# Expert 2's weight loads moved to the end of attention, in a fused attention and top-1 mixture-of-experts kernel

## The chip, the cores and the metric

The kernel runs on one core of a Trainium2 chip. The metric is the device time of one execution in microseconds (us). A profile of one execution is used beside it; its times count from the first instruction, and its span is a little shorter than the device time.

## The reference

Linear attention over 8 batches, 8 heads, 576 positions of 64 values, with an RMS norm; then a mixture of 8 experts in which each of the 4608 tokens goes to one expert.

```python
def _attn_ref(q, k, v, g_norm):
    kv = np.einsum('bhsd,bhse->bhde', k, v)
    out = np.einsum('bhsd,bhde->bhse', q, kv)
    rms = np.sqrt(np.mean(out * out, axis=-1, keepdims=True) + 1e-06)
    return (out / rms * g_norm).astype(np.float32)

def _moe_ref(x, w_gate, w1, w2):          # x: 4608 x 512, w1: 8 x 512 x 1024, w2: 8 x 1024 x 512
    logits = x @ w_gate
    expert_idx = np.argmax(logits, axis=1)
    ...                                   # gate_w: softmax probability of that expert
    for e in range(E):
        mask = expert_idx == e
        h = np.maximum(x[mask] @ w1[e], 0.0)
        out[mask] = gate_w[mask, None] * (h @ w2[e])
    return out
```

Inputs, weights and output are float32.

## The kernel before

Attention runs in 36 steps of 128 tokens. Each finished group of tokens is routed: its rows are scattered by GpSimd to a scratch tensor in HBM, sorted by expert. The experts then gather their rows from there, 128 at a time, transpose them on TensorE (`flip`), multiply by W1 (`one`), apply the ReLU on ScalarE, multiply by W2 (`two`), scale on VectorE (`ys`), and scatter the result rows to the output (`put`).

Experts 0 and 1 are split. Their first three tiles of 128 rows (`Early`, `j0` and `j1`) come from tokens routed early and are gathered before attention ends, through `rowa`. Their other two tiles (`jobs[0]`, `jobs[1]`) and all five tiles of experts 2 to 7 are gathered through `rowi`, which needs every scatter. A last job takes rows beyond the capacity of 608 per expert.

The weights of an expert are 2 MB for W1 and 2 MB for W2 in float32. They are loaded by the queue of SyncE into staging buffers and cast to float16 by `half1` (W1, on ScalarE or VectorE) and `half2` (W2). There is one staging buffer for each of W1 and W2 (`ws1`, `ws2`); expert 1 alone is staged in buffers that the attention inputs k and v leave free (`stage_in`). With `hold`, a one-column memset on VectorE stands before the load, so that the load is issued only when VectorE has come to that place of its program.

```python
        def stage1(self, hold=False):
            self.s1 = P_w.tile([128, 4, F], F32, tag="ws1", bufs=1, name="ws1")
            if hold:
                nc.vector.memset(self.s1[:, 0, 0:1], 0.0)
            nc.sync.dma_start(
                self.s1, moe_w1[self.e, :, :].rearrange("o (t p) f -> p (o t) f", p=128)
            )

        def stage2(self, hold=False):
            self.s2 = P_w.tile([128, 8, D], F32, tag="ws2", bufs=1, name="ws2")
            if hold:
                nc.vector.memset(self.s2[:, 0, 0:1], 0.0)
            nc.sync.dma_start(
                self.s2, moe_w2[self.e, :, :].rearrange("o (t p) d -> p (o t) d", p=128)
            )

        def stage_in(self, pool):

            self.s1, self.s2 = [], []
            for dst, src, tag in ((self.s1, moe_w1, "k"), (self.s2, moe_w2, "v")):
                rows = src[self.e, :, :].rearrange("o (t p) f -> p (o t) f", p=128)
                n = rows.shape[1] // 2
                for m in range(2):
                    t = pool.tile([128, n, rows.shape[2]], F32, tag=tag, bufs=2, name="ws")
                    nc.sync.dma_start(t, rows[:, n * m:n * m + n, :])
                    dst.extend([t[:, kk, :] for kk in range(n)])
...
        def half1(self, eng, kk):     # casts a quarter of W1
...
        def half2(self, kk, eng=None):  # casts a quarter of W2, on ScalarE if no engine is named
...
```

The hooks of the attention steps (`at(last, s, ...)` runs at the end of step `s`):

```python
                for t in range(G):
                    at(last, (33, 34, 34, 35)[t] if g0 == 0 else 35, rt.scatter, t)
                    if g0 == 0 and t == 3:
                        for u in range(AT):
                            at(last, 35, gather_early, 1, u)
        for t in range(AT):
            at(late, 30 + t, gather_early, 0, t)

        at(last, 19, W[0].stage1)
        at(last, 21, W[0].stage2)
        at(last, 30, W[1].stage_in, PA)
        for kk in range(4):
            at(last, (26, 27, 28, 30)[kk], W[0].half1, nc.scalar, kk)
        for kk in range(2):
            at(last, 31 + kk, W[0].half2, kk)

```

The steps, and what follows them:

```python
        j0, j1 = early
        for s in range(36):
            op = x_mm(s)
            for fn in mid[s]:
                fn()
            if s + 2 < 36:
                qt = x_qt(s + 2)
            elif s == 34:
                j0.alloc()
                xp = PSA.tile([128, 2, 1024], F16, tag="kvp", bufs=1, name="xp")
                xp2 = PSA.tile([128, 1024], F16, tag="qtp", bufs=1, name="xp2")
                j0.flip(0, xp[:, 0, :])
                j0.flip(1, xp[:, 1, :])
            else:
                j0.flip(2, xp2)
            rest = x_norm(s, op)
            if s + 2 < 36:
                x_qs(s + 2, qt)
            elif s == 34:
                j0.turned(0, xp[:, 0, :])
                j0.turned(1, xp[:, 1, :])
            else:
                j0.turned(2, xp2)
            for fn in late[s]:
                fn()
            rest()
            for fn in last[s]:
                fn()


        j0.one(0, "op")
        PSA.tile([128, 2, 512], F32, tag="op", bufs=2, name="skipped")
        W[0].half2(2)
        j0.one(1, "kvp")
        j0.one(2, "op")
        W[0].half2(3)
        j0.one(3, "kvp")
        tail.ranks()
        for kk in range(2):
            W[1].half1(nc.scalar, kk)
...
        tail.send()
        for t in range(2):
            tail.scatter(t)
        for t in range(AT):
            j0.where(t)
        yp0 = PSA.tile([128, D], F32, tag="qtp", bufs=1, name="yp")
        j0.two(0, yp0)
...
        j0.done(0, yp0)
        yp = PSA.tile([128, D], F32, tag="misc", bufs=1, name="yp")
        j0.two(1, yp)
        j0.done(1, yp)
        xp = PSA.tile([128, 2, 1024], F16, tag="kvp", bufs=1, name="xp")
        xp2 = PSA.tile([128, 2, 1024], F16, tag="op", bufs=2, name="xp2")[:, 0, :]
        for t in range(AT):
            j1.flip(t, xp[:, t, :] if t < 2 else xp2)
        for t in range(AT):
            j1.turned(t, xp[:, t, :] if t < 2 else xp2)
            j1.where(t)
        W[1].half1(nc.scalar, 2)
        W[1].half1(nc.vector, 3)
        yp = PSA.tile([128, D], F32, tag="qtp", bufs=1, name="yp")
        j0.two(2, yp)
        for t in range(2):
            gather(xe_bufs[2 * AT + t], rowi[:, 0, AT + t:AT + t + 1])
        j0.done(2, yp)
        for t in range(2):
            gather(xe_bufs[2 * AT + 2 + t], rowi[:, 1, AT + t:AT + t + 1])
        W[2].stage1(hold=True)
        W[2].stage2(hold=True)
        for m in range(4):
            j1.one(m, ("op", "kvp")[m % 2])
            if m < 2:
                W[1].half2(m)
        for kk in (2, 3):
            W[1].half2(kk, nc.vector)
```

The jobs:

```python
            def flip(self, t):        # transposes of two tiles, then per tile a copy to xt on VectorE
            ...
            def one(self, ws, f):     # 4 matmuls; every second f a ReLU of two on ScalarE
            ...
            def two(self, t):         # 8 matmuls, then ys on VectorE and put on GpSimd
            ...
        for t in range(AT):
            if t == 2:
                jobs[0].flip(0)
            banks.reverse()
            yp = PSA.tile([128, D], F32, tag=banks[0], bufs=1, name="yp")
            j1.two(t, yp)
            j1.done(t, yp)
        for t in range(CT):
            gather(jobs[2].xe[t], rowi[:, 2, t:t + 1])

        table = left_over_table()
        for n in range(len(order)):
            job = jobs[n]
            nxt = jobs[n + 1] if n + 1 < len(order) else None
            flips = list(range(0, nxt.nt, 2)) if nxt is not None else []

            casts = {0: None, 2: 2, 3: 1, len(order) - 1: None}.get(n, 0)
            coming = list(range(CT)) if 0 < n < len(order) - 3 else []
            if n == 4:
                for _ in table:
            ...
            for ws in range(job.halves):
                for f in range(8):
                    job.one(ws, f)
                    if n in (2, 3):
                        next(table, None)
                    if n == 2 and ws == 0 and f in (3, 7):
                        W[2].half2(2 + f // 4)
                        if f == 7:
                            W[3].stage2()
                    step = 8 * ws + f
                    if coming and (step in (1, 5, 7, 11, 13) if n > 1 else f in (1, 3, 5, 6, 7)):
                        next_row(n + 2, coming.pop(0), job, ws, f)
                    if ws == (0 if n == 3 else job.halves - 1) and f in (2, 4, 6) and flips:
                        nxt.flip(flips.pop(0))
                    if casts == ws and f % 2 == 1:
                        W[n + 1].half1(nc.vector, f // 2)
                        if f == 7 and n + 2 < len(order):
                            W[n + 2].stage1()
            for kk in range(max(job.nt, 4)):
                if kk < job.nt:
                    job.two(kk)
                if casts == 2 and kk < 4:
                    W[n + 1].half1(nc.vector, kk)
                    if kk == 3 and n + 2 < len(order):
                        W[n + 2].stage1()
                if n > 0 and kk < (2 if n == 1 else 4) and nxt is not None:
                    W[n + 1].half2(kk)
                if n > 1 and kk == 3 and n + 2 < len(order):
                    W[n + 2].stage2()
```

[...]

Of the kernel before, what the change touches and what calls it, by code (L numbers as in the profile page):

```python
# [28 lines left out]
def kernel(  # L29
# [11 lines left out]
    nc = tc.nc  # L41
# [102 lines left out]
    class Weights:  # L144
# [11 lines left out]
        def stage2(self, hold=False):  # L156
            self.s2 = P_w.tile([128, 8, D], F32, tag="ws2", bufs=1, name="ws2")
            if hold:
                nc.vector.memset(self.s2[:, 0, 0:1], 0.0)
# [4 lines left out]
        def stage_in(self, pool):  # L164

            self.s1, self.s2 = [], []
            for dst, src, tag in ((self.s1, moe_w1, "k"), (self.s2, moe_w2, "v")):
                rows = src[self.e, :, :].rearrange("o (t p) f -> p (o t) f", p=128)
                n = rows.shape[1] // 2
                for m in range(2):  # L170
                    t = pool.tile([128, n, rows.shape[2]], F32, tag=tag, bufs=2, name="ws")
                    nc.sync.dma_start(t, rows[:, n * m:n * m + n, :])
                    dst.extend([t[:, kk, :] for kk in range(n)])
# [59 lines left out]
    with tc.manual_schedule(engines=by_hand):  # L233
# [402 lines left out]
        for P, g0, G in groups + [(3, 0, 4), (3, 4, 3)]:  # L636
# [11 lines left out]
            else:  # L648
# [4 lines left out]
                for t in range(G):  # L653
                    at(last, (33, 34, 34, 35)[t] if g0 == 0 else 35, rt.scatter, t)
                    if g0 == 0 and t == 3:
                        for u in range(AT):
                            at(last, 35, gather_early, 1, u)
# [5 lines left out]
        at(last, 30, W[1].stage_in, PA)  # L663
# [41 lines left out]
        for s in range(36):  # L705
# [11 lines left out]
            else:  # L717
                j0.flip(2, xp2)
# [6 lines left out]
            else:  # L725
                j0.turned(2, xp2)
# [3 lines left out]
            for fn in last[s]:  # L730
                fn()


        j0.one(0, "op")
        PSA.tile([128, 2, 512], F32, tag="op", bufs=2, name="skipped")
        W[0].half2(2)
        j0.one(1, "kvp")
        j0.one(2, "op")
        W[0].half2(3)
        j0.one(3, "kvp")  # L740
# [39 lines left out]
        W[2].stage1(hold=True)  # L780
        W[2].stage2(hold=True)
# [209 lines left out]
        for t in range(CT):  # L991
            gather(jobs[2].xe[t], rowi[:, 2, t:t + 1])

        table = left_over_table()
        for n in range(len(order)):
# [4 lines left out]
            casts = {0: None, 2: 2, 3: 1, len(order) - 1: None}.get(n, 0)  # L1000
# [6 lines left out]
            for ws in range(job.halves):  # L1007
                for f in range(8):
# [3 lines left out]
                    if n == 2 and ws == 0 and f in (3, 7):  # L1012
                        W[2].half2(2 + f // 4)
                        if f == 7:
                            W[3].stage2()
# [3 lines left out]
                    if ws == (0 if n == 3 else job.halves - 1) and f in (2, 4, 6) and flips:  # L1019
                        nxt.flip(flips.pop(0))  # L1020
# [57 lines left out]
```

## Time and profile before

| | |
|---|---|
| device time, median of 3 runs | 291.94 us (291.26 to 292.26) |
| span of the profiled execution | 284.7 us |
| TensorE matmul (PE) busy | 260.6 us, 92% |
| VectorE (DVE) busy | 162.1 us, 57% |
| ScalarE (ACT) busy | 155.9 us, 55% |
| GpSimd (POOL) busy | 159.3 us, 56% |
| moved by DMA | 85.73 MB, mean 301 GB/s |
| weight loads (SyncE) | 16 of 2048 KB and 4 of 1024 KB, median 11.2 and 11.7 us from issue to landing |

How to read it: the span covers stages with different limits, so a busy share says little of any one of them. The profile cuts the span into 40 slices of about 7.1 us and gives each a digit, the busy share in tenths; "PEclk" is the clock that TensorE was granted, "DMA" the busy share of the 16 DMA engines. In the table of waits a line says which engine and line of the kernel waited for what, with the sum in us, the number of waits and the longest. In a timeline a line gives start and duration in us, engine, line of the kernel, operation, output and input, the count of merged instructions, and in brackets the idle time before them and what ended it. L886 is `flip`, L909 `one`, L928 `two`, L937 `ys`, L182 `half1` on VectorE, L152 and L160 the loads of W1 and W2, L592 the scatter, L199 a gather.

### The profile page before, as it was taken

What the parts mean: (1) busy time and instruction counts of PE and PEld (TensorE: products, weight loads), DVE (VectorE), ACT (ScalarE), POOL (GpSimd) and SP (SyncE); (2) the same over time, 40 slices, a digit from 0 to 9 for tenths busy, and PEclk for the clock granted to TensorE, in tenths of its full rate; (3) what the DMA queues carried; (4) which work ended last, traced back from release to release, by engine and by line L of the source; (5) the groups of instructions that cost most, each with busy time, mean ns of one, the idle gap of its engine ahead of it and who ended that gap; (6) DMA issues with size and microseconds to landing.
All of it is one profiled execution on the core that took longest, in us unless ns stands there. A gap on an engine that the chain in (4) does not pass through costs nothing.

```text
span 284.7 us, 7172 instructions
## 1 busy us (share of the span) xinstructions
PE 260.6 (92%) x2832; PEld 183.9 (65%) x2832; DVE 162.1 (57%) x438; ACT 155.9 (55%) x295; POOL 159.3 (56%) x227
## 2 busy tenths in 40 slices
PE   8979999999999996699889999997979999999992
PEld 3668888888988885545447675673554765746651
DVE  6024677785979778756224767826263545545141
ACT  1135676676666888696503472750736362563721
POOL 3123206666757658877747888874675755124042
PEclk9979999999999999999979999999999999999999
DMA  7999979997999999424994499699999997959222
GB/s 259 373 389 390 391 247 353 327 395 242 397 408 395 396 344 346 162 82 134 341 398 136 135 359 342 219 360 389 385 357 373 328 410 247 398 224 306 115 111 79
DMA packets 34756, 85.73 MB, mean 301 GB/s; under 512 B 3738, under 2 KB 3998, under 8 KB 34721
## 3 DMA queue, kind: packets, MB, share of 16 engines
q1 hardware_dynamic: 26592, 65.10, 63.9%
q0 software_dynamic: 6848, 18.96, 18.0%
q10 hardware_dynamic: 1280, 1.20, 1.3%
q8 instruction: 23, 0.38, 0.5%
q14 instruction: 13, 0.10, 0.1%
HBM read 71.71 MB, written 14.98 MB: 304 GB/s over the span
## 4 chain that ended last, share of the span: by engine, by line
DMA 19%; PE 18%; issue 8%; POOL 5%; DVE 3%; ACT 1%; POOLq 1%; DVEq 0%
DMA ws<-in_moe_w_dram 8%; PE yp L928 8%; DMA out_dram<-ys,idx 8%; PE hp L909 7%; POOL out_dram L216 3%; DMA xe<-xs_scratch,rowi 2%; DVE w1e L182 2%; PE xp L886 2%; POOL xs_scratch L592 1%; PE yp L506 1%; DMA xs_scratch<-xg,sli 1%; DVE xt L890 1%; POOL xe L199 1%; ACT ht L918 0%; POOLq L1073 0%
## 5 line engine op out<-in xcount | busy, mean ns | idle before, releaser
L918 ACT ACTIVATE ht<-hp 128x608 f16<-128x608 f32 (+2 forms) x60 | 38.1, 639 | 60.7 <-PE hp L909 60.7
L216 POOL DMA_INDIRECT out_dram<-ys,idx x41 | 43.1, 1051 | 50.2 <-DVE ys L937 40.1
L928 PE MATMUL yp<-w2e,ht 128*128 128x512 f16 (+1 forms) x280 | 62.1, 379 | 1.9 <-DVE ys L937 1.9
L909 PE MATMUL hp<-xt,w1e 128*128 128x304 f16 (+2 forms) x480 | 62.9, 283 | 0.9 <-ACT ht L918 0.8
L909 PEld LDWEIGHTS <-w1e 128*128 128x128 f16 x480 | 44.9, 98 | 14.3 <-issue 2.0
L928 PEld LDWEIGHTS <-ht 128*128 128x128 f16 (+1 forms) x280 | 28.9, 103 | 32.0 <-issue 2.2
L369 PE MATMUL op<-kvs,qts 128*128 128x144 f32 (+1 forms) x320 | 46.9, 301 | 2.7 <-DVE xg L409 1.7
L937 DVE TENSOR_SCALAR ys<-yp,xe 128x512 f32<-128x512 f32 (+1 forms) x35 | 26.2, 750 | 38.1 <-PE yp L928 38.1
L592 POOL DMA_INDIRECT xs_scratch<-xg,sli x36 | 35.5, 987 | 14.2 <-issue 13.9
L369 PEld LDWEIGHTS op<-kvs,qts 128*128 128x128 f32 (+1 forms) x320 | 38.2, 181 | 5.9 <-DVE xg L409 2.0
L199 POOL DMA_INDIRECT xe<-xs_scratch,rowi x34 | 36.6, 1076 | 9.3 <-issue 4.6
L194 ACT CAST w2e<-ws 128x1024 f16<-128x1024 f32 x32 | 31.5, 1040 | 14.2 <-DMA ws<-in_moe_w_dram 14.2
L395 DVE TENSOR_REDUCE ms<-sq 128x8 f32<-128x512 f32 x36 | 24.6, 684 | 13.9 <-ACT sq L390 13.0
L390 ACT ACTIVATE sq<-op 128x512 f32<-128x512 f32 x36 | 21.4, 594 | 15.3 <-PE op L369 15.3
L283 POOL COPY qp<-q 128x512 f32<-128x512 f32 x32 | 19.3, 616 | 17.0 <-DMA q<-in_q_dram 16.9
L182 DVE TENSOR_SCALAR w1e<-ws,g 128x1024 f16<-128x1024 f32 x29 | 20.5, 748 | 10.5 <-DMA ws<-in_moe_w_dram 10.5
L409 DVE TENSOR_TENSOR xg<-op,rinv 128x512 f16<-128x512 f32 x36 | 24.5, 681 | 0.0
L354 ACT COPY qts<-qtp 128x512 f32<-128x512 f32 x36 | 21.0, 584 | 5.6 <-PE qtp L347 5.4
L347 PE MATMUL qtp<-cf,qp 128*128 128x128 f32 x144 | 22.9, 282 | 0.4 <-issue 0.4
L300 PE MATMUL kvp<-v,k 64*64 64x64 f32 x1152 | 23.2, 225 | 0.0
L890 DVE COPY xt<-xp 128x512 f16<-128x512 f16 x35 | 13.5, 420 | 16.9 <-PE xp L886 16.9
L300 PEld LDWEIGHTS kvp<-v,k 64*64 64x64 f32 x1152 | 19.6, 136 | 5.0 <-issue 5.0
(115 smaller groups left out, 267.4 us busy)
## 6 DMA issues: line engine op xcount, KB each, us to landing
ws<-in_moe_w_dram SPq DMA_DIRECT2D x16, 2048.0 KB, 11.2
q<-in_q_dram SPq DMA_DIRECT2D x8, 1152.0 KB, 13.1
k<-in_k_dram SPq DMA_DIRECT2D x7, 1152.0 KB, 7.6
v<-in_v_dram SPq DMA_DIRECT2D x7, 1152.0 KB, 10.4
ws<-in_moe_w_dram SPq DMA_DIRECT2D x4, 1024.0 KB, 11.7
k<-in_k_dram SPq DMA_DIRECT2D x2, 576.0 KB, 5.2
v<-in_v_dram ACTq DMA_DIRECT2D x2, 576.0 KB, 8.2
out_dram<-ys,idx POOLq DMA_INDIRECT x41, 5.2
```

The lines of the kernel that those rows point to most:

```text
L182: eng.tensor_scalar(self.w1[:, kk, :], st, g2, 1.0, op0=ALU.mult, op1=ALU.mult,)
L194: copy(self.w2[:, 2 * kk:2 * kk + 2, :], self.s2[:, 2 * kk:2 * kk + 2, :])
L199: return nc.gpsimd.indirect_dma_start(out=xe.bitcast(I32), out_offset=None, in_=xs.ap() if src is None else src, in_offset=IndirectOffsetO ...
L216: nc.gpsimd.indirect_dma_start(out=view, out_offset=IndirectOffsetOnAxis(ap=idx, axis=0), in_=ys, in_offset=None, bounds_check=N - 1, oob_ ...
L300: nc.tensor.matmul(kvst[b][64 * ip:64 * ip + 64, c, 64 * i2:64 * i2 + 64], ld["k", b][ps, i, cs], ld["v", b][ps, i, cs], start=(j == 0), s ...
L369: nc.tensor.matmul(op[ts, c, 144 * i2:144 * i2 + 144], qts[s][:, 2 * i2 + c, ts], kvs[:, 2 * c + i2, :], start=True, stop=True,)
L395: nc.vector.reduce_sum(ms, sq, axis=AXX)
L592: put_xs = nc.gpsimd.indirect_dma_start(out=xs_views[9 * self.P + self.g0 + t], out_offset=IndirectOffsetOnAxis(ap=self.sli[:, t:t + 1], a ...
L909: nc.tensor.matmul(self.hp[:, f % 2, 0:wd], self.w.w1[:, kk, f * 128:(f + 1) * 128], self.xt[:, kk, ws * wd:(ws + 1) * wd], start=(kk == 0 ...
L918: nc.scalar.activation(self.ht[f // 4][:, r:r + 2, ws * wd:(ws + 1) * wd], self.hp[:, :, 0:wd], ACTF.Relu,)
L928: nc.tensor.matmul(yp[ps, :], self.ht[f // 4][:, f % 4, t * 128:t * 128 + self.rows[t]], self.w.w2[:, f, :], start=(f == 0), stop=(f == 7),)
L937: nc.vector.tensor_scalar(ys[ps, :], yp[ps, :], self.xe[t][ps, 514:516].bitcast(F32), None, op0=ALU.mult,)
```

## The change

Expert 2's W1 is loaded at the end of step 34 instead of after the gathers of expert 1, and its W2 as soon as the staging buffer is free of expert 0's. To make room, expert 1's W2 is held to the end of step 33, and expert 1's three early gathers go ahead of three scatters. The cast of expert 2's W1 moves from the second part of expert 1 to that of expert 0, so that expert 3's W1 can be loaded during expert 1, behind the gathers of expert 2, which are themselves issued a tile earlier; the later casts and loads move up in the same way. The third transpose group of expert 0's early rows moves from step 35 to the end of step 34, and its four products alternate over the PSUM banks in the other order. The change is meant to use the time in which the DMA engines carry little, at the end of attention and under expert 1.

The diff:

```diff
--- before.py
+++ after.py
@@ -153,24 +153,27 @@
                 self.s1, moe_w1[self.e, :, :].rearrange("o (t p) f -> p (o t) f", p=128)
             )
 
-        def stage2(self, hold=False):
+        def stage2(self):
             self.s2 = P_w.tile([128, 8, D], F32, tag="ws2", bufs=1, name="ws2")
-            if hold:
-                nc.vector.memset(self.s2[:, 0, 0:1], 0.0)
             nc.sync.dma_start(
                 self.s2, moe_w2[self.e, :, :].rearrange("o (t p) d -> p (o t) d", p=128)
             )
 
-        def stage_in(self, pool):
-
-            self.s1, self.s2 = [], []
-            for dst, src, tag in ((self.s1, moe_w1, "k"), (self.s2, moe_w2, "v")):
-                rows = src[self.e, :, :].rearrange("o (t p) f -> p (o t) f", p=128)
-                n = rows.shape[1] // 2
-                for m in range(2):
-                    t = pool.tile([128, n, rows.shape[2]], F32, tag=tag, bufs=2, name="ws")
-                    nc.sync.dma_start(t, rows[:, n * m:n * m + n, :])
-                    dst.extend([t[:, kk, :] for kk in range(n)])
+        def stage_in(self, pool, src, tag, hold=False):
+
+            dst = []
+            rows = src[self.e, :, :].rearrange("o (t p) f -> p (o t) f", p=128)
+            n = rows.shape[1] // 2
+            for m in range(2):
+                t = pool.tile([128, n, rows.shape[2]], F32, tag=tag, bufs=2, name="ws")
+                if hold:
+                    nc.vector.memset(t[:, 0, 0:1], 0.0)
+                nc.sync.dma_start(t, rows[:, n * m:n * m + n, :])
+                dst.extend([t[:, kk, :] for kk in range(n)])
+            if src is moe_w1:
+                self.s1 = dst
+            else:
+                self.s2 = dst
 
         def half1(self, eng, kk):
             if kk == 0:
@@ -652,15 +655,17 @@
                 at(late, s + 2, rt.send)
                 for t in range(G):
                     at(last, (33, 34, 34, 35)[t] if g0 == 0 else 35, rt.scatter, t)
-                    if g0 == 0 and t == 3:
+                    if g0 == 0 and t == 0:
                         for u in range(AT):
-                            at(last, 35, gather_early, 1, u)
+                            at(last, 34, gather_early, 1, u)
         for t in range(AT):
             at(late, 30 + t, gather_early, 0, t)
 
         at(last, 19, W[0].stage1)
         at(last, 21, W[0].stage2)
-        at(last, 30, W[1].stage_in, PA)
+        at(last, 30, W[1].stage_in, PA, moe_w1, "k")
+        at(last, 33, W[1].stage_in, PA, moe_w2, "v", True)
+        at(last, 34, W[2].stage1)
         for kk in range(4):
             at(last, (26, 27, 28, 30)[kk], W[0].half1, nc.scalar, kk)
         for kk in range(2):
@@ -714,30 +719,30 @@
                 xp2 = PSA.tile([128, 1024], F16, tag="qtp", bufs=1, name="xp2")
                 j0.flip(0, xp[:, 0, :])
                 j0.flip(1, xp[:, 1, :])
-            else:
-                j0.flip(2, xp2)
             rest = x_norm(s, op)
             if s + 2 < 36:
                 x_qs(s + 2, qt)
             elif s == 34:
                 j0.turned(0, xp[:, 0, :])
                 j0.turned(1, xp[:, 1, :])
-            else:
-                j0.turned(2, xp2)
             for fn in late[s]:
                 fn()
             rest()
             for fn in last[s]:
                 fn()
-
-
-        j0.one(0, "op")
+            if s == 34:
+                j0.flip(2, xp2)
+                j0.turned(2, xp2)
+
+
+        j0.one(0, "kvp")
+        W[0].half2(2)
+        j0.one(1, "op")
         PSA.tile([128, 2, 512], F32, tag="op", bufs=2, name="skipped")
-        W[0].half2(2)
-        j0.one(1, "kvp")
-        j0.one(2, "op")
+        j0.one(2, "kvp")
         W[0].half2(3)
-        j0.one(3, "kvp")
+        W[2].stage2()
+        j0.one(3, "op")
         tail.ranks()
         for kk in range(2):
             W[1].half1(nc.scalar, kk)
@@ -777,8 +782,6 @@
         j0.done(2, yp)
         for t in range(2):
             gather(xe_bufs[2 * AT + 2 + t], rowi[:, 1, AT + t:AT + t + 1])
-        W[2].stage1(hold=True)
-        W[2].stage2(hold=True)
         for m in range(4):
             j1.one(m, ("op", "kvp")[m % 2])
             if m < 2:
@@ -988,8 +991,9 @@
             yp = PSA.tile([128, D], F32, tag=banks[0], bufs=1, name="yp")
             j1.two(t, yp)
             j1.done(t, yp)
-        for t in range(CT):
-            gather(jobs[2].xe[t], rowi[:, 2, t:t + 1])
+            if t == 1:
+                for u in range(CT):
+                    gather(jobs[2].xe[u], rowi[:, 2, u:u + 1])
 
         table = left_over_table()
         for n in range(len(order)):
@@ -997,7 +1001,8 @@
             nxt = jobs[n + 1] if n + 1 < len(order) else None
             flips = list(range(0, nxt.nt, 2)) if nxt is not None else []
 
-            casts = {0: None, 2: 2, 3: 1, len(order) - 1: None}.get(n, 0)
+            casts = {0: 2, 1: None, len(order) - 1: None}.get(n, 0)
+            wc = 2 if n == 0 else n + 1
             coming = list(range(CT)) if 0 < n < len(order) - 3 else []
             if n == 4:
                 for _ in table:
@@ -1009,29 +1014,25 @@
                     job.one(ws, f)
                     if n in (2, 3):
                         next(table, None)
-                    if n == 2 and ws == 0 and f in (3, 7):
-                        W[2].half2(2 + f // 4)
-                        if f == 7:
-                            W[3].stage2()
                     step = 8 * ws + f
                     if coming and (step in (1, 5, 7, 11, 13) if n > 1 else f in (1, 3, 5, 6, 7)):
                         next_row(n + 2, coming.pop(0), job, ws, f)
-                    if ws == (0 if n == 3 else job.halves - 1) and f in (2, 4, 6) and flips:
+                    if ws == job.halves - 1 and f in (2, 4, 6) and flips:
                         nxt.flip(flips.pop(0))
+                    if n == 1 and f == 3:
+                        W[3].stage1(hold=True)
                     if casts == ws and f % 2 == 1:
-                        W[n + 1].half1(nc.vector, f // 2)
-                        if f == 7 and n + 2 < len(order):
-                            W[n + 2].stage1()
+                        W[wc].half1(nc.vector, f // 2)
+                        if f == 7 and wc + 1 < len(order):
+                            W[wc + 1].stage1()
             for kk in range(max(job.nt, 4)):
                 if kk < job.nt:
                     job.two(kk)
                 if casts == 2 and kk < 4:
-                    W[n + 1].half1(nc.vector, kk)
-                    if kk == 3 and n + 2 < len(order):
-                        W[n + 2].stage1()
-                if n > 0 and kk < (2 if n == 1 else 4) and nxt is not None:
+                    W[wc].half1(nc.vector, kk)
+                if n > 0 and kk < 4 and nxt is not None:
                     W[n + 1].half2(kk)
-                if n > 1 and kk == 3 and n + 2 < len(order):
+                if n > 0 and kk == 3 and n + 2 < len(order):
                     W[n + 2].stage2()
 
     nov = nc.values_load(tabi[0:1, 1, 7:8], min_val=0, max_val=NOV)
```

## The prediction

> **What bounds the kernel now.** I read the page's 40 slices first, then what TensorE waited for, then the time order of TensorE and of the DMA queue of SyncE around each wait, and last the DMA share and the granted clock in short stretches. From the slices of the page (7.1 us each):
>
> ```profile
> PEclk9979999999999999999979999999999999999999
> DMA  7999979997999999424994499699999997959222
> GB/s 259 373 389 390 391 247 353 327 395 242 397 408 395 396 344 346 162 82 134 341 398 136 135 359 342 219 360 389 385 357 373 328 410 247 398 224 306 115 111 79
> ```
>
> The reader is to see two holes in the DMA line: slices 16 to 18 (about 114 to 135 us, 82 to 162 GB/s) and slices 21 and 22 (150 to 164 us, 135 GB/s), each followed by full slices near 390 GB/s. The first hole is the end of attention, the second lies under expert 1. TensorE is busy 92% of the span, so little can be won except where it waits. Its waits from the table of waits, those of the second half:
>
> ```profile
> PE xp L886 <- DMA xe<-xs_scratch,rowi: 2.0, 1, 2.0
> PE yp L928 <- DVE ys L937: 1.9, 1, 1.9
> PE xp L886 <- DVE xt L890: 1.9, 3, 1.5
> PE hp L909 <- ACT ht L918: 0.8, 2, 0.6
> ```
>
> That is 6.6 us between 140 us and the end. Where they lie, from TensorE's timeline:
>
> ```profile
> 143.59 0.90 PE L886 MATMUL xp<-ch,xe 128*128 128x128 f16 x8 [2.00 <-DMA xe<-xs_scratch,rowi]
> 144.34 3.52 PE L506 MATMUL yp<-w2e,early 128*128 128x512 f16 x8
> ...
> 196.65 5.34 PE L928 MATMUL yp<-w2e,ht 128*128 128x512 f16 x24 [1.91 <-DVE ys L937]
> 204.66 3.78 PE L909 MATMUL hp<-xt,w1e 128*128 128x304 f16 x28 [0.60 <-ACT ht L918]
> 211.41 0.61 PE L886 MATMUL xp<-ch,xe 128*128 128x128 f16 x8 [1.49 <-DVE xt L890]
> ```
>
> The eight matmuls at 144.34 took 3.5 us, where the 16 of the same shape at 159.63 took 3.62: half speed. The stretches of 1 us give a granted clock of 1.00 at 143, 0.50 at 145 and 146, and 1.00 again at 148. So the wait at 143.6 costs its 2.0 us and about 1.7 us more. After 215 us the timeline of TensorE has no gap until the leftover tile, so a gain made before 215 us reaches the end undiminished.
>
> The three late waits have one cause, seen on VectorE and in the queue of SyncE:
>
> ```profile
> 193.19 2.74 DVE L182 TENSOR_SCALAR w1e<-ws,g 128x1024 f16<-128x1024 f32 x4 [5.88 <-DMA ws<-in_moe_w_dram]
> 207.86 2.74 DVE L182 TENSOR_SCALAR w1e<-ws,g 128x1024 f16<-128x1024 f32 x4 [4.57 <-DMA ws<-in_moe_w_dram]
> ```
>
> ```profile
> 133.00 0.37 SPq L152 DMA_DIRECT2D ws<-in_moe_w_dram  x1
> 133.47 0.49 SPq L160 DMA_DIRECT2D ws<-in_moe_w_dram  x1
> 160.99 0.37 SPq L152 DMA_DIRECT2D ws<-in_moe_w_dram  x1
> 169.06 0.37 SPq L160 DMA_DIRECT2D ws<-in_moe_w_dram  x1
> 181.52 0.37 SPq L152 DMA_DIRECT2D ws<-in_moe_w_dram  x1
> ```
>
> VectorE sits in a cast of W1 that waits for its load, and the scaling of `ys` and the copies of `xt` queue behind it. The W1 loads of experts 2, 3 and 4 (L152) are issued at 133.0, 161.0 and 181.5: one job late each, as the next stage load waits for the cast that empties the one staging buffer. The chain of loads starts late because expert 2's are held behind a cast of VectorE at 133.
>
> **What the Trainium skill says.** *DMA: Bandwidth & Descriptors*, section "Issuing engines are not separate DMA queues": transfers of SyncE, ScalarE and GpSimd interleave on the same 16 DMA engines. The trace agrees: gathers and scatters that had the engines to themselves landed in 2.8 us (issued at 124.3) and 2.4 us (132.1), while under weight loads they took 5.7 (96.1) and 6.4 us (137.7). The same page, "Rules for kernel authors", says to wait for an earlier DMA's completion before issuing one that reads its bytes; so the row gathers through `rowi` can't be issued before the last scatter has landed. *TensorE: Matmul & The Clock Gate*, Part 1, has an idle TensorE fall to half rate, judged in free-running windows of about 3.4 us; the trace shows that drop after a pause of 2.0 us (and none after 1.91 us at 196.6), so I treat it as chance.
>
> **The change, part by part.** All times are from the span's start.
>
> *End of attention.* Expert 1's W2 was issued with its W1, the last piece at 103.9; now a memset holds it to VectorE's place at the end of step 33, about 117.2 by the old trace (after `lg`, `mx`, `dl` of 116.2 to 117.05). Expert 2's W1 follows at once, its W2 after the cast of expert 0's W2 ends at 125.8. Gather 2 of expert 0's early rows, issued at 110.5, then meets free DMA engines, and the wait of 1.5 us before the transposes at 116.88 goes. In exchange the third transpose group stands ahead of `x_mm(35)`; its gather is issued at 113.8 and took 3.8 us, so 117.6. I put `j0.one(0)` at 119.4 against 119.99 and the end of `j1.two(1)` at 141.1 against 141.6.
>
> *Gathers of the left rows of expert 0.* GpSimd is the pacer: each indirect DMA takes about 1.0 us and 0.3 to the next, and the order change swaps three gathers against scatters without changing how many precede the last scatter, which stays at 132.1. Three loads of 2.1 MB now run from about 118 on. Scatters take about 0.1 MB/us (0.13 MB each 1.3 us) of some 390, leaving 285: by 133.3, 15 us x 0.285 = 4.3 MB of the 6.3 are in. The rest, about 2.0 MB, shares with two result writes of 0.26 MB and is over by about 139. So the last scatter lands not at 134.5 but after 5 to 6 us, at about 137.5; the two gathers are issued at 137.8 and 139.1 (before: 136.3 and 137.7), but the second then meets an almost free DMA and lands at about 142.6 instead of 144.05. The transposes end at about 143.0 instead of 144.5: **-1.5 us**. The pause shrinks and is cut in two; I give the half clock a 40% chance, so of 1.7 us **-1.0** is saved on average.
>
> *Expert 1, second part.* Four casts of expert 2's W1 (0.69 us each in a row) now stand behind expert 0's last tiles. With T the end of these tiles on TensorE (154.9 before), three casts run from T+0.7 to T+2.85, and the first `xt` copy ends at T+3.6. TensorE reaches the second transpose group at T+2.4 and waits 1.2 us, against 0.38 in the two waits of before: **+0.8**.
>
> *Expert 2.* Expert 3's W1 is issued at about T+4.2; the one such load that ran alone among gathers (161.0) had moved its last packet 8.1 us later, so T+12.3; casts to T+15.0. The transposes for expert 3 need VectorE from T+15.2. That is no margin: I allow 0.5 us for lateness, less the wait of 0.21 at 167.59 that goes with ScalarE's two moved casts: **+0.3**.
>
> *Experts 3 and 4.* W4's W1 is issued at about T+15, near 169 instead of 181.5, and every later load follows the cast of the job before, as experts 5 to 7 do already without a wait. In the steady state a job takes 18.15 us (one full job after the next, 222.3 to 240.5) and moves 4.2 + 0.7 + 1.3 = 6.2 MB, 16 us at 390 GB/s. So 1.91 + 0.60 + 1.49 = **-4.0** goes.
>
> Sum: -1.5 - 1.0 + 0.8 + 0.3 - 4.0 = -5.4 us; 291.94 - 5.4 = **286.5 us**.
>
> **The rivals.** (a) *The scatters take over the wait.* If loads still run at 140 us, the gathers land at 144 or later and the half clock returns: then -4.0 + 1.1 and at most -0.5 remain of the sum, about 289. For it: loaded indirect DMAs took 6 us, and 8 MB are to pass from 117 to 138, nearly all that the engines can carry. Against: the second gather has the whole of its flight after the loads. (b) *All waits go.* If scatters land before 136.3 in spite of the loads, TensorE runs through at 141.1 and the transposes end at 142.0: -2.5, the clock -1.7, -4.2 later, +0.8 under expert 1: -7.6, so 284.3. (c) *Expert 3's W1 becomes the new wait.* With 10 to 12 us to landing, as the late loads had when two shared the queue (11.6 at 181.5), TensorE waits 2 to 3.5 us under expert 2, and the result is 289. For it: no margin. Against: expert 3's W2 is issued only at about T+9.8. (d) *The loads were hidden anyway*: the DMA holes are filled but TensorE isn't the gainer, time unchanged. The three late waits, which name the loads, speak against it.
>
> **Range and chances.** The -4.0 is the firm part; (a) and (c) together leave about 291, (b) 284.3, and some 0.7 us either way for what I can't see. Range 283.3 to 290.6. Faster by over 2% means under 286.1, just below the middle of my estimate: 0.44. Within 2%: 0.53. Slower by over 2% (over 297.8) needs a new chain that I don't see: 0.03.
>
> **What would show it.** W1 loads of experts 2, 3 and 4 issued near 118, 158 and 169; no wait of TensorE on `ys` L937 and casts of `w1e` without a DMA wait after 180 us; a DMA share near 1 from 118 to 138; the wait before the first transposes of expert 0's left rows shorter than 2.0 us, no clock of 0.5 after it; a wait of about 1.2 us for `xt` under expert 1. The prediction is wrong if the gathers come later than 144, if W1 of expert 3 lands past T+13, or if the waits on VectorE stay after 190 us.

## The result, and the profile after

The changed kernel takes 287.22 us (median of 4 runs, 286.78 to 288.1), the kernel before in the same set 292.1 us (291.26 to 292.5). The ratio is 0.984, with a 95% interval of 0.9806 to 0.9874: 4.9 us less, against 5.4 predicted.

The two profiles do not show these 4.9 us. Both spans are 284.7 us, and both kernels start expert 5 at the same moment, 222.32 us. The profiled execution of before took 286.55 us, 4.7 to 6.0 us less than the timed ones of its set. So the number came out close to the prediction, and its explanation had to be looked for.

The slices of the profile after, in the form of those shown of before:

```profile
PEclk9999999999999999999999997999999999999998
DMA  7999979998999993499933799799798997959222
```

The first hole is now two slices long and ends at about 121 us instead of 135; slices 17 to 19 are full. The second hole is not filled: it has moved one slice ahead, to slices 20 and 21. The 7 in the clock line has moved from slice 20 (142 to 149 us) to slice 24 (171 to 178 us). TensorE's longest waits in the second half, from the table of waits:

```profile
PE xp L889 <- DVE xt L893: 3.8, 1, 3.8
PE xp L889 <- DMA xe<-xs_scratch,rowi: 3.3, 3, 2.6
```

The waits on `ys` and `ht` are gone (the lines are shifted by three: L889 is `flip`, L893 the copy to `xt`, L185 the cast of W1). But the gathers through `rowi` are waited for longer than the 2.0 us of before, and one new wait of 3.8 us has come. TensorE's timeline has their places:

```profile
143.12 0.40 PE L889 MATMUL xp<-ch,xe 128*128 128x128 f16 x4 [2.55 <-DMA xe<-xs_scratch,rowi]
143.98 0.40 PE L889 MATMUL xp<-ch,xe 128*128 128x128 f16 x4 [0.46 <-DMA xe<-xs_scratch,rowi]
144.21 1.89 PE L509 MATMUL yp<-w2e,early 128*128 128x512 f16 x8
...
157.21 0.61 PE L889 MATMUL xp<-ch,xe 128*128 128x128 f16 x8 [1.26 <-DVE idx L213]
...
173.89 1.01 PE L889 MATMUL xp<-ch,xe 128*128 128x128 f16 x8 [3.75 <-DVE xt L893]
174.70 2.12 PE L912 MATMUL hp<-xt,w1e 128*128 128x304 f16 x8
```

The eight matmuls at 144.21 took 1.89 us, so the half clock after the first wait is gone. It came back at 173.89: the same eight transposes take 0.61 us and the same eight matmuls 1.20 us elsewhere. What the gathers wait for, from GpSimd's timeline (L595 is the scatter, L202 the gather):

```profile
132.96 1.08 POOL L595 DMA_INDIRECT xs_scratch<-xg,sli  x1 [0.30 <-issue]
...
139.88 1.05 POOL L202 DMA_INDIRECT xe<-xs_scratch,rowi  x1 [3.24 <-DMA xs_scratch<-xg,sli]
```

The new wait is explained by VectorE's timeline:

```profile
167.32 0.75 DVE L185 TENSOR_SCALAR w1e<-ws,g 128x1024 f16<-128x1024 f32 x1 [3.29 <-DMA ws<-in_moe_w_dram]
167.99 0.29 DVE L802 TENSOR_SCALAR thr<-cf 128x256 f32<-128x256 f32 x1
...
168.66 0.75 DVE L185 TENSOR_SCALAR w1e<-ws,g 128x1024 f16<-128x1024 f32 x1
...
170.87 0.97 DVE L185 TENSOR_SCALAR w1e<-ws,g 128x1024 f16<-128x1024 f32 x1
...
173.00 0.75 DVE L893 COPY xt<-xp 128x512 f16<-128x512 f16 x2
```

The four casts of expert 3's W1 wait for its load until 167.3 and then stretch to 171.8, because the small steps of the leftover table (L802 and on) stand between them and behind them. The copy to `xt`, for transposes made at 168.5, comes at 173.0. SyncE's queue gives the loads, expert 2's W1 and W2, expert 3's W1, expert 4's W1:

```profile
118.12 0.50 SPq L152 DMA_DIRECT2D ws<-in_moe_w_dram  x1
124.81 0.37 SPq L158 DMA_DIRECT2D ws<-in_moe_w_dram  x1
157.37 0.37 SPq L152 DMA_DIRECT2D ws<-in_moe_w_dram  x1
...
171.87 0.37 SPq L152 DMA_DIRECT2D ws<-in_moe_w_dram  x1
```

### The profile page after: what moved, and what is told of

It is laid out like the page before. It is cut to its first block, busy times and chain, and to the rows that moved or that the text cites. A ratio compares the mean times of both kernels' runs of the same rounds, so it can differ in the third digit from the quotient of the medians.

```text
span 284.7 us, 7174 instructions
## 1 busy us (share of the span) xinstructions
PE 258.8 (91%) x2832; PEld 183.2 (64%) x2832; DVE 161.5 (57%) x439; ACT 156.1 (55%) x295; POOL 159.1 (56%) x227
## 4 chain that ended last, share of the span: by engine, by line
PE 45%; DMA 20%; issue 14%; POOL 8%; DVE 7%; ACT 4%; POOLq 1%; SPq 0%
PE op L372 11%; PE yp L931 10%; PE hp L912 10%; DMA out_dram<-ys,idx 8%; PE kvp L303 5%; DMA xs_scratch<-xg,sli 4%; DMA q<-in_q_dram 4%; DMA ws<-in_moe_w_dram 3%; PE qtp L350 3%; POOL out_dram L219 3%; DVE ms L398 2%; POOL xe L202 2%; PE xp L889 2%; POOL qp L286 2%; DVE w1e L185 2%
## 5 line engine op out<-in xcount | busy, mean ns | idle before, releaser
L219 POOL DMA_INDIRECT out_dram<-ys,idx x41 | 41.9, 1023 | 48.6 <-DVE ys L940 42.7
L372 PE MATMUL op<-kvs,qts 128*128 128x144 f32 (+1 forms) x320 | 46.1, 298 | 2.0 <-DVE xg L412 1.0
L595 POOL DMA_INDIRECT xs_scratch<-xg,sli x36 | 35.9, 998 | 14.1 <-issue 13.0
L202 POOL DMA_INDIRECT xe<-xs_scratch,rowi x34 | 36.2, 1066 | 11.2 <-issue 4.5
L372 PEld LDWEIGHTS op<-kvs,qts 128*128 128x128 f32 (+1 forms) x320 | 37.5, 179 | 5.3 <-DVE kvs L330 2.0
L893 DVE COPY xt<-xp 128x512 f16<-128x512 f16 x35 | 13.5, 419 | 20.8 <-PE xp L889 20.8
L185 DVE TENSOR_SCALAR w1e<-ws,g 128x1024 f16<-128x1024 f32 x29 | 20.9, 760 | 3.3 <-DMA ws<-in_moe_w_dram 3.3
```

Of the source, the lines that this page charges most:

```text
L185: eng.tensor_scalar(self.w1[:, kk, :], st, g2, 1.0, op0=ALU.mult, op1=ALU.mult,)
L202: return nc.gpsimd.indirect_dma_start(out=xe.bitcast(I32), out_offset=None, in_=xs.ap() if src is None else src, in_offset=IndirectOffsetO ...
L219: nc.gpsimd.indirect_dma_start(out=view, out_offset=IndirectOffsetOnAxis(ap=idx, axis=0), in_=ys, in_offset=None, bounds_check=N - 1, oob_ ...
L372: nc.tensor.matmul(op[ts, c, 144 * i2:144 * i2 + 144], qts[s][:, 2 * i2 + c, ts], kvs[:, 2 * c + i2, :], start=True, stop=True,)
L595: put_xs = nc.gpsimd.indirect_dma_start(out=xs_views[9 * self.P + self.g0 + t], out_offset=IndirectOffsetOnAxis(ap=self.sli[:, t:t + 1], a ...
```

## The experiments

Twelve runs in four sets, on three chips; a set has its own runs of the kernel before. The first two sets, e1 to e8, were on one chip on which the kernels took 4 to 6% longer than on the others. I tell those first and briefly, since they settle less.

**e1, the kernel before again.** No edit.

> The kernel before, unchanged, timed and profiled once more. Its first profile had a device time of 286.6 us, but its timed executions took 291.3 to 292.5. Theory A (the 5 us are real work of TensorE that the first profile happened not to show, such as more stretches at half clock or a longer wait before 215 us): timed 291 to 292.5, spans near 290, and if this profile is one of those, a mean clock below 0.987 or waits before 215 us that sum to about 5 us more than 6.6. Theory B (the two differ by the chip or by the way of timing only): timed here about 287 to 288, or a profile of 284.7 again with the same waits.

Measured: 304.5 us (22 runs), before in that set 303.7 (65 runs, 300.0 to 310.3). The same kernel against itself gave a ratio of 1.004 (1.001 to 1.007), so on this chip half a per cent is not told apart. The profile has stops that neither of the two profiles above has; from the timeline of VectorE:

```profile
137.00 0.17 DVE L572 TENSOR_TENSOR t<-pp,oh 128x16 f32<-128x16 f32 x1 [9.65 <-remote]
```

"remote" means that no engine or queue of this core that the profile knows ended the wait. Such stops, of 2 to 12 us, lie between 125 and 175 us in all eight profiles of this chip. They answer neither theory for the 5 us. What they are stays open.

**e2 and e3, the two halves of the change.** e2 keeps the diff up to the removed `stage1(hold=True)` (early loads and gathers, transposes, banks), e3 keeps the rest (gathers of expert 2, casts, later loads):

```diff
 e2:  at(last, 33, W[1].stage_in, PA, moe_w2, "v", True); at(last, 34, W[2].stage1)   # in
      casts = {0: None, 2: 2, 3: 1, ...}                                              # as before
 e3:  W[2].stage1(hold=True); W[2].stage2(hold=True) behind expert 1's gathers        # as before
      casts = {0: 2, 1: None, ...}; W[3].stage1(hold=True) under expert 1             # in
```

> The end-of-attention part of the change alone (early loads of expert 2, early gathers ahead of scatters, transposes moved); the casts of expert 2 and the loads of expert 3 stay where they were. Theory A (the gain comes from the later casts and loads being moved up): the waits behind casts of W1 at about 193 and 208 us stay, and the time is within 1.5 us of before (290.5 to 292.5). Theory B (the early loads are the gain): about 287.

> The other part alone: casts and loads moved up a job, gathers of expert 2 a tile earlier; expert 2's loads held at about 133 us as before. Theory A: expert 2's W1 lands by about 144, so the casts under expert 0 find it there; the waits at 196, 204 and 211 us go (4.0 us), the wait for expert 3's W1 of the changed kernel stays: 286.5 to 288.5. Theory B (the early loads are needed): VectorE waits for expert 2's W1 or the gathers come late, 290 or more.

Measured: ratios 1.004 (1.001 to 1.007) and 0.9945 (0.9905 to 0.9984). The order is that of theory A, but e2 is no further from before than before was from itself, and the expected times can't be tested on this chip. In e2 the wait on `ys` is still there (1.7 us); in e3 it is gone.

**e4, the table steps taken out of expert 2's job.**

```diff
-                    if n in (2, 3):
+                    if n == 3:
                         next(table, None)
```

> The changed kernel with the small VectorE steps of the leftover table taken out of expert 2's job (they run under experts 3 and 4 instead). In the changed kernel they stand between the four casts of expert 3's W1, which took 4.5 us from 167.3 instead of 2.7, and TensorE then waited 3.75 us for the copies to xt and ran 1.3 us at half clock. Theory A (both the late load and the steps between the casts make this wait): the wait shrinks to about 1 us and the half clock goes, 283 to 284.5 us. Theory B (the landing of the load alone sets it): at most 1.5 us less, 285.7 or more.

Measured: 0.9976 (0.9953 to 0.9999), not told apart from the changed kernel of e5 on that chip, so the expected times can't be tested. The mechanism shows: the four casts take 2.9 us in a row (181.46 to 184.31) where e5 has 4.3 (184.78 to 189.08), and the wait for `xt` under expert 2, 1.7 us in e5, is down to 0.3.

**e5, the changed kernel again.** No edit.

> The changed kernel once more, on the chip of this set, beside before. Theory A (its gain is the removed waits behind casts, and the new wait for expert 3's W1 gives most of it back): ratio to before between 0.98 and 1.00, waits behind casts after 190 us absent, a wait for xt of 2 to 4 us under expert 2. Theory B (the gain of 1.6% is a property of one chip): ratio 0.995 to 1.005.

Measured: 0.9994 (0.9949 to 1.0039). On this chip the change brings nothing, which is what theory B allowed, and theory A at its upper end. The wait for `xt` is 1.7 us, below the 2 to 4 of theory A.

**e6, expert 2's W2 alone loaded late.**

```diff
-        W[2].stage2()
         j0.one(3, "op")
...
             if t == 1:
+                W[2].stage2(hold=True)
                 for u in range(CT):
```

> The changed kernel with expert 2's W2 alone moved back, behind the second tile of j1 (about 141 us). Theory A (scatters that land late under the loads set the gathers of expert 0's left rows; in the changed kernel GpSimd waited 3.2 us for them): the wait of GpSimd for the last scatter falls below 1.5 us, that of TensorE from 3.0 to about 1 us, time 1 to 2.5 us below the changed kernel. Theory B (these gathers are paced by GpSimd's own order): unchanged wait, time within 0.7 us of the changed kernel or above it.

Measured: 0.9915 (0.9883 to 0.9947). GpSimd's wait before the first gather through `rowi` fell to 0.3 us, from 2.9 in e5, and the time is about 2.4 us below e5 by the ratios. The last scatter before it landed 2.5 us after its issue, by the completions that the trace records for it, and 6.0 us in e5. So the loads are what delays these gathers: theory A. TensorE's waits don't test it, since in neither profile is one put down to these rows.

**e7, expert 2's W1 cast early.** The float16 W1 of expert 2 goes into the four `kvs` buffers that attention has left, before expert 0's left rows; expert 3's W1 is then loaded under expert 0.

```diff
+                if self is W[2]:
+                    self.w1 = [
+                        PA.tile([128, F], F16, tag=f"kvs{n}", name="w1k") for n in range(4)
+                    ]
...
         for kk in (2, 3):
             W[1].half2(kk, nc.vector)
+        for kk in range(4):
+            W[2].half1(nc.vector, kk)
...
-            casts = {0: 2, 1: None, len(order) - 1: None}.get(n, 0)
+            casts = {0: None, 1: None, len(order) - 1: None}.get(n, 0)
...
-                    if n == 1 and f == 3:
+                    if n == 0 and f == 3:
                         W[3].stage1(hold=True)
```

> The changed kernel with expert 2's W1 cast before expert 0's left rows (into space that attention leaves free) and expert 3's W1 loaded at about 148 instead of 157 us. Theory A (the late landing of expert 3's W1 and the row of casts under expert 1 make the waits for xt): waits for xt of 1.3 and 3.75 us and the half clock after the second go, 5 to 6.5 us below the changed kernel. Theory B (the wait moves: the load then meets the gathers of experts 1 and 2, which come later): 0 to 3 us below.

**e8, e4, e6 and e7 together.**

> Both of these moves, and the small steps of the leftover table taken out of expert 2's job. Theory A (the causes add up): 7 to 9 us below the changed kernel, no wait of TensorE above 1 us after 145 us. Theory B (they share one resource, the DMA engines between 118 and 160 us, so that one eats the other's gain): no better than the better one of the two alone by more than 1 us.

Measured: e7 0.9925 (0.9892 to 0.9958), e8 0.9851 (0.9796 to 0.9907). Each median lies below that of e5, e8 lowest, 298.6 us against 305.0; the interval of e7 still touches that of e5. By the ratios e7 is about 2 us below e5, as its theory B has it, and e8 about 4, less than the 7 to 9 of its theory A. The intervals of e6, e7 and e8 overlap, so how the gains add is not told.

**e9, e10 and e11: before, change and combination on another chip.** No new edit; e11 is the kernel of e8.

> The kernel before, unchanged, in one set with the change and the combined version. On the first chip its timed runs were 5 us slower than its profiled one; on the second chip engines stood still for 2 to 10 us at a time between 125 and 170 us, in waits that no engine or queue of this core ended. Theory A (those stops depend on the chip and the moment and explain the 5 us too): spans that spread with the number of such stops, and this profile has stops if its span is above 288. Theory B (the 5 us are waits behind casts and loads): a profile above 288 has waits of TensorE on ys, xt and ht beyond 6.6 us, with no such stops.

> The changed kernel beside it. Theory A: without stops its span equals that of before within 1 us (284 to 286), and the ratio of timed runs lies between 0.985 and 1.005 as the stops fall. Theory B: 0.98 to 0.987 again.

> The combined version (expert 2's W2 loaded at about 141 us, its W1 cast early, table steps later) in the same set. Theory A (late scatters, late W1 of expert 3 and the row of casts cost the changed kernel 8 to 9 us): 6 to 9 us below the changed kernel where no stops come in, span near 277. Theory B (the DMA engines are the common limit): 3 us or less.

Here the case opened. The 39 runs of before fall in two groups with nothing between: 9 at 284.9 to 288.2 us and 30 at 290.3 to 293.6 (median of all 290.95). The 20 runs of the change lie at 285.3 to 289.2 (median 287.37), in one group. (The ratios of this set and the next are formed with the faster group alone, so the change has 1.0028, interval 0.9986 to 1.007; I give the medians beside them.) The granted clock doesn't tell the two groups apart: it is 0.977 to 1.0 in the faster and 0.971 to 0.988 in the slower one. The profile of e9 is one of the slower group, span 290.2. Neither theory fits it: it has none of the stops of the other chip, and its waits on `ys`, `xt` and `ht` sum to 4.4 us, no more than the 4.6 of the first profile. The time is lost elsewhere, as TensorE's timeline shows:

```profile
146.99 0.61 PE L886 MATMUL xp<-ch,xe 128*128 128x128 f16 x4 [4.70 <-DMA xe<-xs_scratch,rowi]
148.67 0.61 PE L886 MATMUL xp<-ch,xe 128*128 128x128 f16 x4 [1.07 <-DMA xe<-xs_scratch,rowi]
149.07 3.62 PE L506 MATMUL yp<-w2e,early 128*128 128x512 f16 x8
```

The wait for expert 0's left rows is 5.8 us instead of 2.0, and the half clock follows it. What GpSimd does before it, first in the first profile of before, then in e9 (L592 is a scatter, L199 a gather):

```profile
130.83 0.96 POOL L592 DMA_INDIRECT xs_scratch<-xg,sli  x1 [0.30 <-issue]
132.09 0.96 POOL L592 DMA_INDIRECT xs_scratch<-xg,sli  x1 [0.30 <-issue]
...
136.33 1.04 POOL L199 DMA_INDIRECT xe<-xs_scratch,rowi  x1 [0.55 <-issue]
```

```profile
131.57 1.50 POOL L592 DMA_INDIRECT xs_scratch<-xg,sli  x1 [0.30 <-issue]
133.38 1.02 POOL L592 DMA_INDIRECT xs_scratch<-xg,sli  x1 [0.30 <-issue]
...
141.16 1.04 POOL L199 DMA_INDIRECT xe<-xs_scratch,rowi  x1 [4.03 <-issue]
```

And SyncE's queue in e9:

```profile
133.69 0.37 SPq L152 DMA_DIRECT2D ws<-in_moe_w_dram  x1
134.16 0.45 SPq L160 DMA_DIRECT2D ws<-in_moe_w_dram  x1
```

In the faster execution the last scatter starts at 132.09, 0.9 us ahead of expert 2's loads (133.00). In the slower one the last but one takes 1.5 us, the last starts at 133.38, 0.3 us ahead of the loads (133.69), and GpSimd doesn't go on to the gather until 141.2. A delay of 1.3 us has become one of 4.8. The timeline doesn't name what ended GpSimd's wait in e9 ("issue"), but the trace also records the completions of each DMA, 16 for every scatter here, and the last of the 16 tells when the scatter had landed:

| profile | last scatter issued | first load of expert 2 issued | scatter landed | gather issued |
|---|---|---|---|---|
| before, first profile | 132.09 | 133.00 | 135.55, after 3.5 us | 136.33 |
| before, e9 | 133.38 | 133.69 | 140.38, after 7.0 us | 141.16 |
| change, first profile | 132.96 | 118.12 | 139.11, after 6.2 us | 139.88 |

In all three the gather is issued 0.8 us after the landing, so in e9 too GpSimd waited for the scatter. In e9 the two gathers then met the same loads and landed 5.8 and 6.1 us after their issue; in the changed kernel, where the loads are nearly over by then, they took 3.2 and 2.7 us. The profile of e1 fits as well: there the last scatter was issued 6 us ahead of the loads (141.78 and 148.02), its last recorded completion came after 2.7 us, and TensorE didn't wait for expert 0's left rows. If that one profile is typical of its chip, before had no such delay to lose there, and the change nothing to gain.

The profile of e10, the change again, has span 286.5 and repeats the change's first: GpSimd waits 3.3 us for the scatter, TensorE 3.8 us for `xt`.

e11 has a median of 286.09 us (20 runs, 284.05 to 287.63; against the faster group 1.0002, 0.9968 to 1.0036): the fastest of the three on this chip, but 1.3 us below the change and not 6 to 9. Expert 2's job took 18.1 us, where the change's first profile has 23.2, and no wait for `xt` is above 0.2 us: that part of theory A held. A new wait took the place, and the half clock followed it. From TensorE's timeline, then GpSimd's and SyncE's (L901 is `flip`, L213 the gather):

```profile
149.98 1.04 PE L901 MATMUL xp<-ch,xe 128*128 128x128 f16 x8 [4.85 <-DMA xe<-xs_scratch,rowi]
```

```profile
141.67 1.02 POOL L213 DMA_INDIRECT xe<-xs_scratch,rowi  x1 [0.31 <-issue]
```

```profile
141.17 0.37 SPq L160 DMA_DIRECT2D ws<-in_moe_w_dram  x1
```

Expert 2's W2, moved to 141.2, ran into the gathers of expert 1's left rows (141.67 and 143.00), which now landed 8.3 and 7.2 us after issue. Theory B was right in that: here too the loads and the small transfers share the DMA engines. The combination of e7's casts and e4's table with the early W2 loads of the change, which these readings point to, was not run.

**e12, before with its loads behind the gathers.** This tests the cause of the two groups. One edit: expert 2's loads wait for GpSimd to have issued expert 0's two gathers.

```diff
             if hold:
-                nc.vector.memset(self.s1[:, 0, 0:1], 0.0)
+                nc.gpsimd.memset(self.s1[:, 0, 0:1], 0.0)
...                                                          # s2 likewise
         for t in range(2):
             gather(xe_bufs[2 * AT + t], rowi[:, 0, AT + t:AT + t + 1])
+        W[2].stage1(hold=True)
+        W[2].stage2(hold=True)
...
-        W[2].stage1(hold=True)
-        W[2].stage2(hold=True)
```

> The kernel before with one edit: expert 2's two loads wait for GpSimd to have issued the gathers of expert 0's left rows (a memset on GpSimd behind them), not for VectorE at 133 us. Theory A (in most runs of before the last scatter meets these loads, lands 4 us late and holds up GpSimd and with it the gathers; in the rest it lands just ahead of them): the slow group of 290 to 293.5 us goes, all runs at 285.5 to 288.5, GpSimd waits under 1 us for the scatter and TensorE under 1.5 us for the first of these gathers. Theory B (the two groups come from something else, such as the clock): both groups stay.

Measured, on the third chip of the experiments: 286.98 us (8 runs, 285.9 to 289.1), before 291.26 (11 runs: 4 at 285.8 to 286.6, 7 at 291.1 to 292.2; ratio to the four 1.0042, 0.9989 to 1.0096). The slower group is gone: none of 8 runs, against 7 of 11 beside them. GpSimd's timeline, then TensorE's:

```profile
132.74 0.96 POOL L592 DMA_INDIRECT xs_scratch<-xg,sli  x1 [0.30 <-DMA xs_scratch<-xg,sli]
...
136.80 1.04 POOL L199 DMA_INDIRECT xe<-xs_scratch,rowi  x1 [0.30 <-issue]
```

```profile
142.19 0.61 PE L886 MATMUL xp<-ch,xe 128*128 128x128 f16 x8
142.64 1.89 PE L506 MATMUL yp<-w2e,early 128*128 128x512 f16 x8
...
147.13 0.40 PE L886 MATMUL xp<-ch,xe 128*128 128x128 f16 x4 [1.45 <-DMA xe<-xs_scratch,rowi]
```

The last scatter landed after 2.5 us, and there is no wait for it and none for expert 0's rows. The two waits for expert 1's rows, 1.9 us together (147.13 and 147.98), and two of 0.8 us together for expert 2's are the price, as the loads (139.30 and 139.76) now meet those gathers. That is theory A. This one edit leaves the later waits behind casts in place (1.4 us on `ys`, 1.9 on `xt`) and lies 4.3 us below the median of before on its chip; the whole change lies 4.9 and 3.6 us below in two other sets. The two were not timed in one set.

## Why the prediction was right in its number and wrong in its way

**The base.** I took 291.94 us from the timed runs and the waits from a profile of an execution of 286.55 us. They belong to two different courses of the same kernel: in the slower one the last scatter meets expert 2's loads and lands after 7.0 us, in the faster it is far enough ahead of them to land after 3.5. I had the time and the span of 284.7 side by side and didn't ask about the 7 us between them, of which the profiled execution itself has only 1.9. From its own 286.55 the sum of -5.4 would have meant 281. Against that profile the change gained nothing (284.7 both). That the number came out right is luck: the sum of -5.4, of other waits, happened to equal the 5.5 us between the two courses (spans 290.2 and 284.7).

Against e9, the typical course, the change's first profile is 5.5 us shorter: 1.7 until `j0.one` starts, 2.1 from there to the first gathered rows, 2.7 to the first product of expert 0's left rows (second gather and half clock), 0.1 up to expert 1's second part, then 0.9 and 4.7 lost under experts 1 and 2, and 4.5 won under experts 3 and 4.

By the steps, change against first profile of before, each measured from the start of one part to that of the next:

| step | predicted | measured |
|---|---|---|
| start of `j0.one`, end of `j1.two` | 119.4, 141.1 | 118.9, 140.6 |
| transposes of expert 0's left rows end | 143.0 (-1.5) | 144.4 (-0.1) |
| half clock behind them | -1.0 on average | gone, -1.6 |
| rows of expert 1 behind expert 0's | not in the sum | wait of 0.32 for a gather, +0.4 |
| expert 1: row of casts | +0.8 | 1.43 instead of 0.38, +1.05 |
| expert 2: late W1 | +0.3 | wait of 3.75 and half clock, +4.7 |
| experts 3 and 4 | -4.0 | waits gone, -4.4 |

These sum to zero within rounding, and the spans are equal.

*Gathers.* The step that put the last scatter's landing at about 137.5 failed. It was issued at 132.96 instead of 132.1 and took 6.2 us instead of 5 to 6, so it landed at 139.11, and GpSimd issued the first gather at 139.88, 2.1 us later than predicted. What followed went as argued: the loads were nearly over (the DMA engines are full at 139 us and 57% busy at 141), and the gathers landed 3.2 and 2.7 us after issue, just ahead of 144. Rival (a) was right that loads still run at 140, and wrong that the half clock returns. The base of this step was misread too: the scatter of before issued at 132.1 did not land after 2.4 us, at 134.5, but after 3.5, at 135.55 (the table under e9).

*Expert 2* is the term that was mis-sized. W1 was issued at 157.37, 3.8 us after T (4.2 predicted), but landed 9.9 us later, not 8.1: T+13.7, past the T+13 that the prediction names as a sign of being wrong. Part of this is in the 8.1 itself, which counts to the load's last packet; the last completion that the trace records for that load came after 8.8. The casts took 4.5 us, not 2.7, for I had left out the table steps, although the code lists them (`next(table, None)` for n in 2 and 3) and the timeline of before shows them. So `xt` was copied 4.5 us after the transposes. This is rival (c), above the size I gave it. e11, in which expert 3's W1 is loaded 5 us earlier and the table steps are moved, has none of it; e4 shows that the steps alone stretch the casts. The two causes were not told apart in time.

*Experts 3 and 4* went as argued: loads follow the cast of the job before, and no cast waits for a DMA after 180 us. One of the three waits had another source than VectorE: the 0.6 us for `ht` at 204.66 stood behind ScalarE's casts of W2, which had waited for their load until 200.15. It went all the same.

**Where the measured 4.9 us are from.** From the race between the last scatter and expert 2's loads, which the change ends by issuing the loads far ahead, not from the step I called firm: e12 ends the race alone and gains 4.3 us. The 4.4 us of the late casts are won, and given back under expert 2. That each slower timed run of before has the course of e9 is inferred from one trace and from e12's single group; why the last but one scatter took 1.5 us in e9, so that the last came closer to the loads, stays open.

## What to carry to other kernels

Before pricing a change from a profile, compare the profiled execution's own time with the timed runs: 5 us between them meant another course of the kernel here, and the terms of the sum came from the wrong one. Where a small transfer that others wait for is issued within a microsecond of a large load, order the two explicitly, by letting the load wait for it; a memset on the issuing engine, behind its gathers and ahead of each load, gained 4.3 us here, the whole rearrangement 3.6 and 4.9. When a load is moved, list every small transfer that will be in flight with it: each move here (to 118, 139 and 141 us) freed some small transfers and delayed others.

## What the runs showed that I had not expected

A scatter of 128 rows of 1 KB landed in 2.5 us with no load near (e12), in 3.5 us when it was issued 0.9 us ahead of 4 MB of loads, and in 7.0 us when it was 0.3 us ahead (e9). The length of a pause alone did not decide the clock of TensorE: it fell to half after pauses of 2.0 and 3.75 us and not after two of 2.55 and 0.46 us; and in e12 it was 0.50 from 117 to 120 us behind a pause of 1.5 us that left it at 1.00 in the first profile of before. On one chip before took about 12 us more and the change about 18, with engines standing for 2 to 12 us on events that the profile can't place, and there the change was worth nothing (0.9994, 0.9949 to 1.0039).
